# Linear attention into an expert layer on one core: q transposed for two chunks at once, kv in both partition halves, a new order by unit, and two weight semaphores

## The chip, the cores and the metric

The kernel runs on one core of a Trainium2 chip. Times are device microseconds (us) of that core. A program is run several times; runs of one kernel mostly agree within a per cent. A run is called slow when it lies more than 1.5% above the fastest run of the same kernel, and comparisons use fast runs. A single run has no known state, and is used here only for differences well above that. Engines are named as the profile names them: PE is the tensor engine, PEld its weight loads, DVE the vector engine, ACT the scalar engine, POOL the GpSimd engine, SP the engine that issues most loads. In the views, `qo` is a q product, `qtp` the transposes of q and `qT` their copy, `kvp` a k product, `kvc` the evicted kv and `kvtp` its transpose, `kt` and `vtl` the tails of k and v, `wt` the buffer that holds most other tiles, `hp` and `yps` the first and the second layer of an expert tile.

## The reference

```python
# attention: 8 batches, 8 heads, 576 positions, 64 wide, float32
r = relu(x);  phi(x) = concat(r * cos(theta_pos), r * sin(theta_pos))
kv  = einsum('bhsf,bhsd->bhfd', phi(k), v);   z = sum over s of phi(k)
x   = phi(q) @ kv / (phi(q) . z + 1e-6)        # rows: 4608 of 512
# experts: 8, hidden 1024; every row goes to one expert
logits = x @ w_gate;  e = argmax(logits);  gate = softmax(logits)[e]
out[row] = gate * sigmoid(x @ w_output_gate)[e] * (relu(x @ w1[e]) @ w2[e])
```

## The kernel before

The attention part runs over 36 units: a batch has four chunks of 128 positions, and each pair of batches shares a ninth unit for the tails. A group is one such pair, nine units. While the q products of a batch run, k and v of the next one are worked into `kv`. Rows are scattered to their expert's region in memory as the groups end. After that 43 expert tiles of 128 rows follow, each with two layers; the expert of a tile is read from a table into a register.

```python
def load_w(r):                      # weights of the expert ranked r, issued by POOL
    er = GP.value_load(ordi[0:1, r:r + 1], min_val=0, max_val=E - 1)
    if r > 0:
        GP.wait_ge(wsem, 32 * r)    # until all earlier ones have landed
    for d in (GP.dma_start(w1v[:, r], ...), GP.dma_start(w2v[:, r], ...)):
        d.then_inc(wsem, 16)

def k_prep(b, c):                   # k and v step c of batch b
    DVE.tensor_copy(vc[:, :, 0:D], vbuf[b % 2][:, :, c, :])
    ACT.activation(kc[:, 0], src, AF.Relu, scale=cosc[:, c:c + 1])
    DVE.tensor_scalar(kc[:, 1], src, sinc[:, c:c + 1], 0.0, ALU.mult, ALU.max)

def q_prep(b, c):                   # relu of q, heads rearranged
    ACT.activation(qr..., src..., AF.Relu)

def q_tr(b, c):                     # four transposes, one PSUM copy
    ...
    ACT.copy(qT, tp[:])

def layer1(j):                      # expert tile j
    ev = PE.value_load(tcol(0, j), min_val=0, max_val=7)
    wv = PE.value_load(tcol(1, j), min_val=32, max_val=256)
    PE.wait_ge(wsem, wv)
    ...                             # 8 matmuls of 512 columns
    ACT.activation(hs[:], hp, AF.Relu)

for i, (b, c) in enumerate(units):
    q_mm(b, c, ...)
    q_tr(next unit)
    ...                             # k_prep and k_mm of batch b + 1
    if c == len(plan) - 1:          # eviction and transpose at once
        gst["kvc"] = g_evac(b + 1)
        gst["kvT"] = g_tr(b + 1, gst["kvc"])
    elif c == len(plan):
        g_mm(b + 1, gst["kvT"])
        k_prep(b + 2, 0)
    ...
    if c == 2:                      # loads on SP's queue
        load_q(b + 2); load_k(b + 3); load_v(b + 3)
        # even b: also load_tails(g + 1)
```

Of the kernel before, what the change touches and what calls it, by code (L numbers as in the profile page):

```python
# [21 lines left out]
def kernel(  # L22
# [12 lines left out]
    PE = nc.tensor  # L35
# [79 lines left out]
    for qd in range(4):  # L115
        hA = 4 * (qd // 2) + qd % 2
        for ab in range(2):
            h = hA + 2 * ab
            DVE.tensor_copy(wpr[0:64, qd, 32 * ab:32 * ab + 16], wg0[0:64, h, :])
            DVE.tensor_copy(wpr[64:128, qd, 32 * ab + 16:32 * ab + 32],  # L120
                            wg0[64:128, h, :])
# [49 lines left out]
    wsem = tc.alloc_semaphore("wsem")  # L171
    ordi = constp.tile([P, E], I32, name="ordi")

    def load_w(r):
        er = GP.value_load(ordi[0:1, r:r + 1], min_val=0, max_val=E - 1)
        if r > 0:

            GP.wait_ge(wsem, 32 * r)
        for d in (GP.dma_start(w1v[:, r], moe_w1[bass.ds(er, 1)].rearrange(
                      "o (c p) f -> p (o c) f", p=128)),  # L180
                  GP.dma_start(w2v[:, r], moe_w2[bass.ds(er, 1)].rearrange(
                      "o (c p) d2 -> p (o c) d2", p=128))):
            d.then_inc(wsem, 16)
            tc.declare_no_dep(d.ins, group="mm", reason="ranks loaded before")
            tc.add_to_no_dep_group("w", d.ins)
# [16 lines left out]
    r_kvm = Rot(5, 0, 3, 648)  # L202
    r_kc = Rot(5, 2 * 3 * 648, 2, 1024)
    r_u = Rot(6, 0, 2, 1296)
    r_qr = Rot(6, 2 * 2 * 1296, 2, 512)
    r_t = Rot(7, 0, 2, 324)
    r_qT = Rot(7, 2 * 2 * 324, 2, 512)
    r_kvT = Rot(7, 2 * (2 * 324 + 2 * 512), 1, 512)
    r_v = Rot(7, 2 * (2 * 324 + 3 * 512), 3, 520)
# [6 lines left out]
    tabs = [[constp.tile([P, n], I32, name=f"tab{i}_{m}") for m in range(3)]  # L216
# [13 lines left out]
    if True:  # L230
# [6 lines left out]
        tails, kvps, kvms, kcs, qrs, qTs, us, vcs = {}, {}, {}, {}, {}, {}, {}, {}  # L237
# [35 lines left out]
        def k_prep(b, c):  # L273
# [3 lines left out]
            if c < 4:  # L277
                kc = r_kc().rearrange("p (s h d) -> p s h d", s=2, h=H)
                vc = r_v().rearrange("p (h d) -> p h d", d=65)
                DVE.tensor_copy(vc[:, :, 0:D], vbuf[b % 2][:, :, c, :])  # L280
# [10 lines left out]
        def k_mm(b, c):  # L291
# [7 lines left out]
            for hf in range(2):  # L299
                for pr in range(2):  # L300
                    for cs in range(2):
                        for ab in range(2):
                            h = 4 * hf + pr + 2 * ab
                            o = 130 * pr + 65 * cs
                            PE.matmul(kvp[64 * ab:64 * ab + 64, hf, o:o + 65],  # L305
                                      kc[p0:p1, cs, h, :], vc[p0:p1, h, :],
                                      start=(c == 0 and pr == 0 and cs == 0),
                                      stop=(c == 4), skip_group_check=True)


        def g_evac(b):
            kvp = kvps[b]
            kvm = r_kvm().rearrange("p (a w) -> p a w", w=81)
            kvms[b] = kvm
            DVE.tensor_copy(kvm[:, 0:4, 0:65],
                            kvp[:, 0, 0:260].rearrange("p (a w) -> p a w", w=65))
            ACT.copy(kvm[:, 4:8, 0:65],
                     kvp[:, 1, 0:260].rearrange("p (a w) -> p a w", w=65))
            kvc = wk.tile([P, 8, 64], F32, name=f"kvc{b}", tag="kvc", bufs=1)
            DVE.tensor_copy(kvc[:], kvm[:, :, 0:64])  # L320
            return kvc

        def g_tr(b, kvc):
# [5 lines left out]
            kvT = r_kvT()  # L329
            ACT.copy(kvT, tp[:])  # L330
            return kvT.rearrange("p (q w) -> p q w", q=4)

        def g_mm(b, kvT):
            gp = ptr.tile([P, 512], F32, name=f"kvgp{b}", tag="tr")
            for qd in range(4):
                for ab in range(2):
# [4 lines left out]
            DVE.tensor_copy(kvms[b][:, :, 65:81],  # L341
                            gp[:, 0:128].rearrange("p (q w) -> p q w", w=16))


        def q_prep(b, c):
            src = qbuf[b % 2][:, :, c, :] if c < 4 else tails[b // 2, "q"][:]

            qr = r_qr()
            ACT.activation(qr.rearrange("p (r a d) -> p r a d", r=2, a=4),
                           src.rearrange("p (a r) d -> p r a d", r=2), AF.Relu)  # L350
            qrs[b, c] = qr

        def q_tr(b, c):
            qrf = qrs.pop((b, c))
            tp = ptr.tile([P, 512], F32, name=f"qtp{b}_{c}", tag="tr")
            for i in range(4):
                PE.transpose(tp[:, 128 * i:128 * i + 128],  # L357
                             qrf[:, 128 * i:128 * i + 128], ident[:])
            qT = r_qT()
            ACT.copy(qT, tp[:])  # L360
            qTs[b, c] = qT.rearrange("p (q w) -> p q w", q=4)

        def q_mm(b, c, u):
            g = b // 2
            qT = qTs.pop((b, c))
            for hf in range(2):
                qo = pqo.tile([P, 4, 256], F32, name=f"qo{b}_{c}_{hf}", tag="qo")
                for pr in range(2):
                    qd = 2 * hf + pr
                    for ab in range(2):  # L370
                        r0 = 64 * ab
                        lhs = qT[r0:r0 + 64, 2 * pr + hf, :]
                        if c < 4:
                            PE.matmul(qo[:, 2 * ab + pr, 0:162], lhs,  # L374
                                      kvms[b][r0:r0 + 64, 2 * qd:2 * qd + 2, :],
                                      start=True, stop=True)
                        else:
                            for i in range(2):
                                PE.matmul(qo[64 * i:64 * i + 64, 2 * ab + pr, 0:162],
                                          lhs[:, 64 * i:64 * i + 64],  # L380
                                          kvms[2 * g + i][r0:r0 + 64,
# [445 lines left out]
```

## Time and profile before

| | before |
|---|---|
| time, median of 2 runs | 433.11 us (431.85 to 434.36) |
| span of the profiled run (a third run, of 437.43 us), mean granted clock | 435.8 us, 0.913 |
| last q product starts | 195.37 us |
| first expert product starts | 210.73 us |
| last first-layer product starts | 421.97 us |
| median distance of two expert tiles | 4.58 us |

The page of the profile cuts the span into 40 slices, here of 10.9 us. A digit is the busy share of a slice in tenths; the row PEclk is the granted clock of the tensor engine in tenths; the last row is what the DMA engines moved.

```profile
PE   0478988795867799570656989899887999999992
PEclk9999989895998859966596999999999999999997
GB/s 178 298 321 246 245 278 53 318 75 335 39 205 158 159 151 117 184 142 162 121 48 108 129 201 188 191 236 152 185 197 217 74 97 83 53 96 36 50 11 0
```

The reader is to see two regimes. Up to slice 18 is attention with full-clock and cold slices mixed; from slice 23 to slice 39 PE is busy 7 to 9 tenths of the time, mostly 8 or 9, with the granted clock at 9 tenths or more.

### The profile page before, as it was taken

Reading aid. Unit: us, or ns where it says so; the run is one execution under the profiler, and the core shown is the slowest. Engines: PE = TensorE matmul, PEld = TensorE weight load, DVE = VectorE, ACT = ScalarE, POOL = GpSimd, SP = SyncE. Lnnn points to the kernel's source line nnn. Section 1 sums busy time; section 2 is a strip of 40 time slices with the busy share of each in tenths; the row PEclk is TensorE's granted clock in tenths of the full one; section 3 lists DMA queues with packets and bytes.
Section 4 is the critical chain, followed back from the end, with each engine's and each line's share of the span. In section 5 each row is a group of like instructions: output and inputs, shape, how many; then the busy total and the mean of one; then the engine's idle time right before and its main releaser. Section 6 shows DMA issues by size and latency. Waiting matters only on the chain.

```text
span 435.8 us, 9962 instructions
## 1 busy us (share of the span) xinstructions
PE 335.8 (77%) x3468; PEld 222.3 (51%) x3468; DVE 215.3 (49%) x619; ACT 154.5 (35%) x248; POOL 140.8 (32%) x177
## 2 busy tenths in 40 slices
PE   0478988795867799570656989899887999999992
PEld 0467766674756677450323544444444544545441
DVE  4444848574877557773354343343333433433421
ACT  1355767473746467551110212112211112122120
POOL 2001213176314853475343323304241121221211
PEclk9999989895998859966596999999999999999997
DMA  6997892939166587977413699897996232120100
GB/s 178 298 321 246 245 278 53 318 75 335 39 205 158 159 151 117 184 142 162 121 48 108 129 201 188 191 236 152 185 197 217 74 97 83 53 96 36 50 11 0
DMA packets 65374, 66.86 MB, mean 153 GB/s; under 512 B 18350, under 2 KB 57774, under 8 KB 65328
## 3 DMA queue, kind: packets, MB, share of 16 engines
q0 software_dynamic: 17712, 30.98, 32.5%
q1 hardware_dynamic: 47616, 35.25, 29.2%
q8 instruction: 31, 0.51, 0.5%
q14 instruction: 15, 0.12, 0.1%
HBM read 67.61 MB, written 17.22 MB: 195 GB/s over the span
## 4 chain that ended last, share of the span: by engine, by line
DMA 36%; issue 25%; PE 15%; POOL 9%; DVE 7%; SPq 3%; ACT 2%; POOLq 1%; another core or an unknown queue 0%; DVEq 0%; ACTq 0%
DMA xs<-xr,di@1_1635 11%; DMA out_dram<-ysb,sidx 7%; POOL out_dram L666 6%; DMA out_dram<-ysb,xg 6%; PE kvp L305 5%; PE qo L374 4%; DMA xs<-xr,di@3_2587 4%; DMA wt<-in_v_dram 4%; PE qtp L357 2%; POOL xs L467 2%; PE hp L640 2%; DVE wt L386 1%; DMA xs<-xr,di@2_2206 1%; SPq L759 1%; PE kvtp L327 1%
## 5 line engine op out<-in xcount | busy, mean ns | idle before, releaser
L646 ACT ACTIVATE hs<-hp 128x1024 f16<-128x1024 f32 x43 | 44.0, 1023 | 171.4 <-PE hp L640 171.4
L640 PE MATMUL hp<-wt,xts 128*128 x344 | 84.3, 388 | 15.4 <-issue 11.3
L662 DVE TENSOR_SCALAR ysb<-yps,xg 128x512 f32<-128x512 f32 x43 | 32.3, 751 | 128.3 <-PE yps L655 116.7
L655 PE MATMUL yps<-wt,hts 128*128 x344 | 83.0, 385 | 12.4 <-DVE xts L610 8.3
L395 POOL TENSOR_TENSOR xr<-wt,rc 128x1024 f16<-128x1024 f32 (+1 forms) x20 | 37.8, 1890 | 110.2 <-DVE rc L394 105.8
L666 POOL DMA_INDIRECT out_dram<-ysb,sidx x35 | 34.7, 993 | 94.8 <-DVE ysb L662 92.4
L655 PEld LDWEIGHTS <-hts 128*128 128x128 f16 x344 | 33.9, 99 | 54.4 <-DVE xts L610 8.7
L374 PE MATMUL qo<-wt 64*128 64x162 f32 x512 | 51.3, 346 | 12.1 <-DVE wt L386 8.4
L640 PEld LDWEIGHTS <-xts 128*128 128x128 f16 x344 | 33.9, 99 | 51.7 <-issue 18.5
L386 DVE SCALAR_TENSOR_TENSOR wt<-qo,sinc,wt 128x324 f32<-128x324 f32 x72 | 38.4, 553 | 38.0 <-ACT wt L385 36.1
L305 PE MATMUL kvp<-wt 128*64 128x65 f32 x1024 | 40.3, 237 | 20.3 <-ACT wt L288 18.1
L374 PEld LDWEIGHTS qo<-wt 64*128 64x128 f32 x512 | 42.6, 213 | 16.9 <-issue 7.9
L305 PEld LDWEIGHTS kvp<-wt 128*64 128x64 f32 x1024 | 35.9, 149 | 24.6 <-issue 20.8
L385 ACT ACTIVATE wt<-qo,cosc 128x324 f32<-128x324 f32 x72 | 37.7, 530 | 29.9 <-PE qo L374 19.4
L625 DVE COPY hts<-htsp 128x1024 f16<-128x1024 f16 x43 | 29.3, 683 | 1.5 <-issue 1.5
L622 PE MATMUL htsp<-ident,hs 128*128 128x128 f16 x344 | 26.7, 221 | 1.3 <-issue 0.7
L357 PE MATMUL qtp<-ident,wt 128*128 128x128 f32 x144 | 27.5, 321 | 0.0
L288 ACT ACTIVATE wt<-wt,cosc 128x512 f32<-128x512 f32 x32 | 22.5, 722 | 9.2 <-DVE cosc L100 5.1
L607 PE MATMUL xtsp<-ident,xg 128*128 128x128 f16 x172 | 17.5, 227 | 10.7 <-DMA xg<-xs 10.7
L607 PEld LDWEIGHTS <-xg 128*128 128x128 f16 x172 | 13.7, 102 | 21.3 <-DMA xg<-xs 11.0
L610 DVE COPY xts<-xtsp 128x512 f16<-128x512 f16 x43 | 17.9, 416 | 10.9 <-PE xtsp L607 7.5
L360 ACT COPY wt<-qtp 128x512 f32<-128x512 f32 x36 | 21.1, 585 | 5.1 <-PE qtp L357 4.1
(239 smaller groups left out, 327.5 us busy)
## 6 DMA issues: line engine op xcount, KB each, us to landing
wt<-in_moe_w_dram POOLq DMA_DIRECT2D x16, 1024.0 KB
wt<-in_k_dram SPq DMA_DIRECT2D x16, 512.0 KB, 7.1
wt<-in_v_dram SPq DMA_DIRECT2D x16, 512.0 KB, 7.0
wt<-in_q_dram SPq DMA_DIRECT2D x16, 512.0 KB, 6.0
xg<-xs SPq DMA_DIRECT2D x43, 129.0 KB, 2.1
xs<-zt SPq DMA_DIRECT2D x9, 129.0 KB, 3.6
kt<-in_k_dram SPq DMA_DIRECT2D x8, 128.0 KB, 10.1
vtl<-in_v_dram SPq DMA_DIRECT2D x8, 128.0 KB, 6.3
```

The lines of the kernel that those rows point to most:

```text
L305: PE.matmul(kvp[64 * ab:64 * ab + 64, hf, o:o + 65], kc[p0:p1, cs, h, :], vc[p0:p1, h, :], start=(c == 0 and pr == 0 and cs == 0), stop=(c ...
L357: PE.transpose(tp[:, 128 * i:128 * i + 128], qrf[:, 128 * i:128 * i + 128], ident[:])
L374: PE.matmul(qo[:, 2 * ab + pr, 0:162], lhs, kvms[b][r0:r0 + 64, 2 * qd:2 * qd + 2, :], start=True, stop=True)
L385: ACT.activation(t, qo[:, :, 0:81], AF.Copy, scale=cosc[:, c:c + 1])
L386: DVE.scalar_tensor_tensor(u[:, 4 * hf:4 * hf + 4, :], qo[:, :, 81:162], sinc[:, c:c + 1], t, ALU.mult, ALU.add)
L395: GP.tensor_tensor(xr[:, 0:n, 0:DM].bitcast(F16).rearrange("p n (h d) -> p n h d", d=D), u[:, 0:m, 0:64].rearrange("p (n h) d -> p n h d", ...
L607: PE.transpose(xp16[:, kc * 128:(kc + 1) * 128], xg[:, kc * 128:(kc + 1) * 128].bitcast(F16), ident16[:, :])
L640: mm = PE.matmul(hp[:, fh * 512:fh * 512 + 512], xts[:, kc, :], wt[:, bass.ds(ev, 1), kc * F + fh * 512:kc * F + fh * 512 + 512], start=(k ...
L646: ACT.activation(hs[:], hp, AF.Relu)
L655: mm = PE.matmul(yp, hts[:, fc, :], wt[:, bass.ds(ev, 1), 4 * F + fc * DM:4 * F + fc * DM + DM], start=(fc == 0), stop=(fc == 7))
L662: DVE.tensor_scalar(ysb[:], yp, xg[:, DM + 2:DM + 4].bitcast(F32), None, ALU.mult)
L666: d = GP.indirect_dma_start(out=out[:, :], out_offset=bass.IndirectOffsetOnAxis(ap=idx, axis=0), in_=ysb[:], in_offset=None, bounds_check= ...
```

## The change

It has six intents. Relu of q moves into the PSUM copy behind the transposes, which now take two chunks from q's own layout, so one of two ACT passes goes. For that, `kv` must lie in both halves of the partitions, and two DMA copies per batch put it there. The copy of v moves from DVE to ACT. The order by unit changes, so that the eviction of kv ends a unit before its transpose. The late table of the experts is cut into parts. And weights count on two semaphores, so that POOL waits for the last load but one. Smaller edits, such as the places where weights are loaded, are in the kernel but not in these cuts.

```diff
-            GP.wait_ge(wsem, 32 * r)
+            GP.wait_ge(wsem[r % 2], 16 + 32 * ((r - 1) // 2))
...
-                DVE.tensor_copy(vc[:, :, 0:D], vbuf[b % 2][:, :, c, :])
+                ACT.copy(vc[:, :, 0:D], vbuf[b % 2][:, :, c, :])
...
+            SP.dma_start(kvd[0:64, 8:16, :], kvd[64:128, 0:8, :])
+            SP.dma_start(kvd[64:128, 8:16, :], kvd[0:64, 0:8, :])
...
-        def q_prep(b, c):
...
-            ACT.copy(qT, tp[:])
+            ACT.activation(qT[:].rearrange("p q w -> p (q w)"), tp[:], AF.Relu)
...
             ev = PE.value_load(tcol(0, j), min_val=0, max_val=7)
-            wv = PE.value_load(tcol(1, j), min_val=32, max_val=256)
-            PE.wait_ge(wsem, wv)
+            wv = PE.value_load(tcol(1, j), min_val=16, max_val=112)
+            PE.wait_ge(wsem[0], wv)
+            wv = PE.value_load(tcol(3, j), min_val=16, max_val=144)
+            PE.wait_ge(wsem[1], wv)
...
+        kplan = {0: [(1, 1), (1, 2)], 1: [(1, 3), (1, 4), (1, "evac")],
+                 2: [(1, "tr"), (1, "mm")], 3: [(2, 0)], 4: [(2, 1)],
+                 5: [(2, 2), (2, 3)], 6: [(2, 4), (2, "evac")],
+                 7: [(2, "tr"), (2, "mm")], 8: [(3, 0)]}
...
+        def prep_next():            # prepares the step after the one in hand
+            if flat:
+                k_prep(*flat.pop(0))
...
+        k_prep(1, 0)
+        k_do(0, "evac")
+        k_do(0, "tr")
+        q_tr(0)
+        k_do(0, "mm")               # ends with the two copies
+        k_mm(1, 0)
+        prep_next()
...
+            ks = [w for _, w in steps[i] if isinstance(w, int)]
+            if ks:
+                prep_next()
...
+            q_mm(i, u)
+            if i + 1 < NU:
+                q_tr(i + 1)
+            for m, (kb, w) in enumerate(steps[i]):
+                if isinstance(w, int) and w != ks[0]:
+                    prep_next()
+                k_do(kb, w)
...
+            if n in (2, 6):         # n is the unit in its group
+                load_q(bb + 2); load_k(bb + 3); load_v(bb + 3)
+                if n == 2: load_tails(g + 1)
```

## The prediction

> **What bounds the kernel now.** I first cut the span into stretches with the view of windows: the four head-and-batch groups of the attention part (nine chunks each, two batches per group), the hand-over to the experts, and two halves of the expert part.
>
> ```profile
> core 0: us, PE busy (x) PEld busy (x) DVE busy (x) ACT busy (x) POOL busy (x), PEclk, DMA share, GB/s
> 27.90:67.20 39.30, 33.73 (x556) 28.50 (x557) 23.94 (x59) 27.18 (x50) 8.06 (x4) 0.91 0.93 268
> 67.20:114.40 47.20, 36.71 (x566) 30.36 (x566) 31.04 (x82) 27.33 (x52) 20.85 (x24) 0.86 0.61 179
> 114.40:162.00 47.60, 38.12 (x566) 31.86 (x566) 32.43 (x95) 26.81 (x52) 22.89 (x27) 0.82 0.56 149
> 162.00:197.00 35.00, 26.38 (x382) 21.57 (x382) 26.27 (x88) 20.84 (x40) 18.83 (x22) 0.90 0.88 151
> 197.00:237.00 40.00, 18.21 (x92) 8.88 (x93) 17.85 (x67) 4.07 (x6) 16.95 (x26) 0.66 0.40 106
> ```
>
> PE is the busiest engine of every attention group, but the same work (556 to 566 matmul records) costs 39.3 us in one group and 47 in the next two, and the granted clock falls with it. The hand-over at 197 to 237 holds only 18 us of PE work. So PE order bounds the kernel, through its gaps and the slow clock after them. The timeline of PE shows one such gap in the first group:
>
> ```profile
> 38.51 1.15 PE L305 MATMUL kvp<-vtl,ktc 64*64 64x65 f32 x32
> 41.16 0.63 PE L327 MATMUL kvtp<-ident,kvc 128*128 128x128 f32 x4 [1.49 <-DVE kvc L320]
> 41.71 2.17 PE L374 MATMUL qo<-wt 64*128 64x162 f32 x16
> 43.81 1.11 PE L357 MATMUL qtp<-ident,wt 128*128 128x128 f32 x4
> 44.86 0.95 PE L337 MATMUL kvgp<-wpr,wt 128*64 128x32 f32 x16
> 46.30 1.37 PE L374 MATMUL qo<-wt 64*128 64x162 f32 x16 [0.49 <-DVE wt L341]
> ```
>
> PE waits 1.49 us for the eviction of kv, then the next q product takes 2.17 us against 1.37, and its two followers 1.11 and 0.95 against 0.66. That happens once per batch. The hand-over, from the same view (start, duration, engine, line, operation, tiles, count, and in brackets the wait before it):
>
> ```profile
> 195.37 1.34 PE L379 MATMUL qo<-wt 64*64 64x162 f32 x32 [0.67 <-ACT wt L360]
> 207.41 0.61 PE L607 MATMUL xtsp<-ident,xg 128*128 128x128 f16 x4 [10.70 <-DMA xg<-xs]
> ...
> 210.73 3.57 PE L640 MATMUL hp<-wt,xts 128*128 x8 [1.04 <-DVE den@3_2565 L453]
> ...
> 222.74 1.89 PE L640 MATMUL hp<-wt,xts 128*128 x8 [0.22 <-issue]
> ...
> 232.93 3.57 PE L655 MATMUL yps<-wt,hts 128*128 x8 [8.30 <-DVE xts L610]
> ...
> 237.16 1.89 PE L640 MATMUL hp<-wt,xts 128*128 x8
> ...
> 241.73 1.89 PE L640 MATMUL hp<-wt,xts 128*128 x8 [0.29 <-issue]
> ```
>
> PE stands 10.7 us for the first gathered rows (their scatter sits behind an expert's weights), then 8.3 us behind the late table on DVE. In steady state a slot of 128 rows takes 241.73 - 237.16 = 4.57 us. Between the products at 237.16 and 421.97 lie 39 slots, 184.8 us, 4.74 each: 6.6 us of losses. The waits of POOL say where from:
>
> ```profile
> POOL wt L179 <- DMA out_dram<-ysb,sidx: 10.6, 1, 10.6
> POOL wt L179 <- DMA xs<-xr,di@1_1635: 7.6, 1, 7.6
> POOL wt L179 <- DMA out_dram<-ysb,xg: 7.2, 1, 7.2
> ```
>
> POOL blocks before an expert load until the previous one has landed, and scatters and outputs queue up behind it.
>
> **What the Trainium skill says.** "TensorE: Matmul & The Clock Gate", Part 1, says the array runs at half rate after an idle window of about 3.4 us and at full rate again after one busy window. The trace agrees in size (2.17 against 1.37 us, about 3.5 us long), but gaps of only 1.4 to 1.5 us already precede it here. "DMA: Bandwidth & Descriptors", Queues, rings and completion order, says an issuing engine has one ring per DMA engine, consumed in order. The trace agrees: a gather on an empty queue lands in 2.1 us, a v load behind q and k takes a median of 7.0. The first page's specification table calls the ACT, DVE and POOL queues strict FIFO, so program order decides there.
>
> **The change part by part.**
>
> 1. Relu of q moves into the PSUM copy: 32 x 623 ns + 4 x 632 ns = 22.5 us of ACT go. The v copy moves to ACT, 32 instructions; I take the removed 623 ns for the same shape, so 19.9 us come back. DVE loses 32 x 430 ns = 13.8 us. ACT is level: about 28 us per group, against PE's pure work. That work I get from the windows: a mean clock of 0.91 means 18% of the time at half rate, so 39.3 x 0.09 = 3.5 us of the busy 33.7 is slowness, 30.2 remain; likewise 36.7 - 6.6 = 30.1 and 38.1 - 8.6 = 29.5. So 30 us per group. Matmul and transpose counts do not change.
>
> 2. Order. Eviction of kv now stands at the end of a unit, its transpose after the next unit's q product and q transposes (1.31 + 0.59 = 1.9 us of PE work, against the chain of 1.45). So eight gaps of about 1.45 us, 11.6 us, go, and most of the cold stretch after each (0.8 + 0.5 + 0.3 = 1.6 us in the one above). Within the unit of kv transpose and gate product a wait of about 1 us stays, since ACT must do two evictions and the relu first. With about 3 us of small waits, I put a group at 35 to 36 us, the last (one batch of k fewer) at 32.
>
> 3. Two SP copies of kv per batch are new, and q products of odd heads wait for both. On an empty queue: issue 0.5 each plus 2.1 landing plus semaphores, about 3.5 us. They have one unit (3.0 to 3.2 us) to hide in, so 0.5 us per batch is exposed. But they share SP's queue with the loads. At the start, from the timeline of SP:
>
> ```profile
> 21.20 3.10 SPq L242 DMA_DIRECT2D wt<-in_q_dram  x2
> 24.43 2.30 SPq L242 DMA_DIRECT2D wt<-in_k_dram  x2
> 26.78 2.20 SPq L242 DMA_DIRECT2D wt<-in_v_dram  x2
> ```
>
> The first copies come after these, at about 29.3 us, and behind v's bytes (issue plus about 7), so they land near 35.5. First q product: 27.9 before, about 35.6 after; one k product is done meanwhile, so 6.5 us are lost, and a cold restart of 1.5. At later group boundaries the copies stand behind q, k and v of later batches. From the second such burst before (issued from 75.3, drained about 88) I expect landing 12 us after the burst begins, while its unit and the two units after it give about 7.5: 4.5 to 5 us lost at the second boundary, 8 at the first, where nine zero fills (7 us of SP) also stand ahead. At the third only q is left to load; I put 0.5.
>
> 4. Hand-over. Scatters of group 2 now end around unit 33, and the third expert load stands after them, so the first gather can be issued before attention ends. After the last q product I count evictions 1.7, small divisions 1.0, first row copy 0.5, routing to the one-hot 1.8, ranks 0.5: 5.5 us until the first expert product instead of 210.7 - 196.7 = 14.0. Gain 8.5.
>
> 5. The late table is cut over three slots. Per slot PE gives DVE 2.8 us between two second-layer products, of which 2.05 are its own work (0.42 + 0.68 + 0.75 for the two row copies and the output scaling, 0.2 for semaphores), so parts of 3.1, 2.3 and 4.9 us (sums of the row durations) stall PE by 2.3, 1.5 and 4.1: 8 us. Before, 237.16 - 222.74 = 14.4 for one slot, nearly 10 over the pace. Gain near 2 to 3, with the cold stretch.
>
> 6. Weight semaphores: a load waits for the last but one. POOL stops blocking; of 6.6 us lost I give back 5. The third load is also later, still far ahead of its first slot.
>
> Sum, as a time line: first q product 35.6, groups begin near 77, 118 and 154, last q product ends near 186.5 (196.7 before). From there to the end 239 us before; minus 8.5, 2.5 and 5, and about 2 for startup copies I do not see in detail, 221. That gives 407.5 in the profile against 435.8. The median of the timed runs is 433.1 for that profile, 2.7 less, so about 405.
>
> **The rivals.** First, the copies behind loads become the new bound: speaking for it, DMA share 0.93 in group one and the full queue at 21 to 34 us; against it, later groups have share 0.6. If stalls were twice mine, attention would gain nothing and the time would be 420. Second, the reverse: copies slip through and the loads are idle anyway. Then attention ends near 172 and the time is 392. Third, ACT takes PE's place: 28 of 30 us per group, and both halves of a q product now finish together, so evictions begin late. If each of 36 units loses 0.5 us more, that is 18 us: 423. Against it, ACT rows issued back to back start 0.48 to 0.55 us apart, less than their durations. Fourth, the earlier expert start runs into weights not landed: each takes about 16 us (two loads released 16.4 us apart), and loads are now spaced 3 to 4 slots, 14 to 18 us, so outputs queue behind them; five output buffers give 23 us. I allow 3 us.
>
> **Range and chances.** The gain in the hand-over and weights (16 to 18 us, 4%) needs little from attention; attention is 10 us of gain with an error of 12 either way. So 405, 8 in 10 between 391 and 419. Faster by over 2% (below 424.4) 0.92, within 2% 0.07, slower 0.01.
>
> **What would show it.** The kv transpose no longer waits for the eviction; clock per group above 0.93; q products wait for a DMA of kv at the start for about 7 us and at two boundaries for 4 to 8; first expert product 5 to 7 us after the last q product; no POOL wait before weight loads; PE waiting for DVE three times in slots 1 to 4. Wrong would be: q products waiting on ACT or DVE in most units, no wait on the copies, or expert products waiting for weights.

## More of the kernel before

The view of one tile's instructions shows who reads the tables of the experts (count, duration in ns as minimum, median, maximum, and the first and last start in us), here in a window of two expert tiles.

```profile
L629 PEldq TENSOR_LOAD <-tab x2: 300/304/308, 342.3 to 346.9; - x2
L630 PEldq TENSOR_LOAD <-tab x2: 301/304/307, 343.0 to 347.6; - x2
```

PE's own sequencer loads two registers per tile. Each is recorded as 0.30 us, but the second starts 0.70 us after the first.

## The result, and the profile after

The changed kernel takes 488.87 us (488.23 and 489.5), the kernel before 433.11 us: it is slower by 13%. The ratio is 1.1287, with a 95% interval of 1.1133 to 1.1442. Ratios here are the mean time of one kernel's fast runs over the mean of the other's of the same rounds, so not quite the ratio of the medians. The profiled span went from 435.8 to 486.6 us, the granted clock from 0.913 to 0.878.

| stretch of the profiled run | before | after | difference |
|---|---|---|---|
| start to the start of the last q product | 195.37 | 228.09 | +32.7 |
| from there to the first expert product | 15.4 | 11.4 | -4.0 |
| from there to the last first-layer product | 211.2 | 233.1 | +21.9 |
| from there to the end | 13.8 | 14.0 | +0.2 |

So two stretches lost time, one of them the expert part, for which the prediction had only gains. The page after:

```profile
PE   0547857689597677877486777887887788788783
PEclk9977997588799958855568899999999999999999
GB/s 190 297 295 9 141 262 280 58 43 319 316 65 88 337 182 133 9 178 114 109 167 126 76 149 179 177 209 164 185 156 198 111 83 66 55 91 44 43 10 0
```

The expert part stands at 7 and 8 tenths where it was at 8 and 9, at full clock. In attention the DMA row now swings between 9 and 337 GB/s: the loads come in bursts with silence between them. Before, slice 4 of 40 moved 246 GB/s, now 9.

The waits of PE, in all, number of times and longest, from the view of waits:

```profile
PE hp L654 <- issue: 30.2, 30, 1.2
PE kvp L303 <- ACT wt L288: 16.0, 1, 16.0
PE qo L375 <- DMA wt<-wt: 15.0, 3, 6.1
PE kvp L303 <- DMA vtl<-in_v_dram: 11.5, 2, 5.8
...
PE kvtp L326 <- DVE kvc L319: 6.0, 1, 6.0
```

The top line is the expert part: 30 first-layer products were not held by any engine or transfer that the profile shows ("issue"), for a microsecond each. The single 16 us is the start of the program, and is there before the change too. The third, fourth and last are attention: q products that wait for the new copies (`wt<-wt`), k products that wait for the tails of v, and the first kv transpose.

The tables, in a window of two expert tiles, answer the top line:

```profile
L641 PEldq TENSOR_LOAD <-tab x2: 297/300/303, 380.7 to 386.1; - x2
L642 PEldq TENSOR_LOAD <-tab x2: 299/300/302, 381.4 to 386.8; - x2
L644 PEldq TENSOR_LOAD <-tab x2: 295/295/295, 382.1 to 387.5; - x2
```

Each tile now loads three registers, 0.70 us apart, and the products stand behind the last one. From the timeline of PE in the same window (the figure in brackets is the idle time before the first product):

```profile
383.04 1.89 PE L654 MATMUL hp<-wt,xts 128*128 x8 [1.11 <-issue]
...
388.26 1.89 PE L654 MATMUL hp<-wt,xts 128*128 x8 [0.94 <-issue]
```

Before, the same idle time was 0.28 us:

```profile
343.84 1.89 PE L640 MATMUL hp<-wt,xts 128*128 x8 [0.29 <-issue]
...
348.40 1.89 PE L640 MATMUL hp<-wt,xts 128*128 x8 [0.28 <-issue]
```

The Trainium skill, "DMA: Bandwidth & Descriptors", Latency and other measured facts, gives a floor of some 600 ns for a `tensor_load`; 0.70 us from start to start on PE agrees in size; the record of 0.30 us alone does not.

Now SP, in the first group of attention:

```profile
32.20 0.54 SPq L343 DMA_DIRECT2D wt<-wt  x1
...
53.90 0.46 SPq L343 DMA_DIRECT2D wt<-wt  x1
54.40 0.60 SPq L344 DMA_DIRECT2D wt<-wt  x1
55.10 1.14 SPq L242 DMA_DIRECT2D wt<-in_q_dram  x2
56.29 3.15 SPq L242 DMA_DIRECT2D wt<-in_k_dram  x2
59.48 2.15 SPq L242 DMA_DIRECT2D wt<-in_v_dram  x2
61.67 2.80 SPq L258 DMA_DIRECT2D kt<-in_k_dram  x2
64.52 3.40 SPq L261 DMA_DIRECT2D vtl<-in_v_dram  x2
```

From 33.4 to 53.9 us SP issues nothing, because the next instruction in its queue is a copy whose source is not ready. The loads behind it leave at 55.1, where the corresponding ones left from 36.02 us on before the change (not all of that is the copy's doing: see "Copies issued by ACT"); the tails, the last of them, leave at 61.7 to 67.9 and are wanted at 65.9. PE then waits 5.63 us for them, and its first product after that takes 2.00 us, where the same 32 took 1.15. This happens in three groups:

```profile
71.61 2.00 PE L303 MATMUL kvp<-vtl,ktc 64*64 64x65 f32 x32 [5.63 <-DMA vtl<-in_v_dram]
...
89.17 2.49 PE L375 MATMUL qo<-wt,qT 64*128 64x162 f32 x14 [6.07 <-DMA wt<-wt]
...
126.48 2.00 PE L303 MATMUL kvp<-vtl,ktc 64*64 64x65 f32 x32 [5.82 <-DMA vtl<-in_v_dram]
...
172.30 2.00 PE L303 MATMUL kvp<-vtl,ktc 64*64 64x65 f32 x32 [5.80 <-ACT ktc L288]
```

The last of these names ACT, which itself waited for the tail of k.

At the start, ACT stood 5.82 us, until 26.81, for v of batch 1. The eviction of kv of batch 0 was queued behind that, and so were the kv transpose and the first copies.

### The profile page after: what moved, and what is told of

The parts are those of the page before. It is cut to its first block, busy times and chain, and to the rows that moved or that the text cites. A ratio compares the mean times of both kernels' runs of the same rounds, so it can differ in the third digit from the quotient of the medians.

```text
span 486.6 us, 10013 instructions
## 1 busy us (share of the span) xinstructions
PE 353.6 (73%) x3468; PEld 238.5 (49%) x3468; DVE 203.5 (42%) x589; ACT 147.5 (30%) x244; POOL 134.6 (28%) x145
## 4 chain that ended last, share of the span: by engine, by line
issue 29%; DMA 24%; PE 16%; SPq 10%; POOL 8%; DVE 7%; ACT 3%; POOLq 1%; ACTq 0%; DVEq 0%
PE qo L375 8%; POOL out_dram L680 6%; DMA out_dram<-ysb,xg 5%; SPq L242 5%; DMA out_dram<-ysb,sidx 5%; DMA wt<-wt 4%; PE kvp L303 4%; DMA wt<-in_moe_w_dram 3%; PE qtp L358 2%; DMA wt<-in_v_dram 2%; DMA kt<-in_k_dram 2%; SPq L258 2%; DMA vtl<-in_v_dram 2%; DVE wt L390 2%; SPq L261 1%
## 5 line engine op out<-in xcount | busy, mean ns | idle before, releaser
L375 PE MATMUL qo<-wt,qT 64*128 64x162 f32 x512 | 62.8, 375 | 22.2 <-DMA wt<-wt 15.0
L375 PEld LDWEIGHTS qo<-wt,qT 64*128 64x128 f32 x512 | 51.7, 235 | 27.7 <-issue 12.4
L390 DVE SCALAR_TENSOR_TENSOR wt<-qo,sinc,wt 128x324 f32<-128x324 f32 x72 | 36.6, 549 | 49.1 <-ACT wt L387 49.0
L387 ACT ACTIVATE wt<-qo,cosc 128x324 f32<-128x324 f32 x72 | 34.3, 526 | 61.3 <-PE qo L375 54.5
L303 PEld LDWEIGHTS kvp<-wt 128*64 128x64 f32 x1024 | 37.7, 159 | 20.0 <-issue 20.0
L358 PE MATMUL qtp<-ident,wt 128*128 128x128 f32 x128 | 25.2, 329 | 0.0
L303 PE MATMUL kvp<-vtl,ktc 64*64 64x65 f32 x256 | 11.7, 256 | 17.3 <-DMA vtl<-in_v_dram 11.5
L289 DVE TENSOR_SCALAR wt<-wt,sinc 128x512 f32<-128x512 f32 x32 | 15.8, 493 | 18.9 <-PE kvp L303 18.7
L360 ACT ACTIVATE qT<-qtp 128x512 f32<-128x512 f32 x36 | 21.5, 596 | 3.9 <-PE qtp L358 3.7
L634 PEld LDWEIGHTS <-hs 128*128 128x128 f16 x344 | 21.8, 100 | 1.4 <-ACT hs L660 1.0
```

The source lines that it names most:

```text
L303: PE.matmul(kvp[64 * ab:64 * ab + 64, s_ // 2, o:o + 65], kc[p0:p1, cs, 2 * s_ + ab, :], vc[p0:p1, 2 * s_ + ab, :], start=(c == 0 and s_ % ...
L358: PE.transpose(tp[:, 128 * m:128 * m + 128], src, ident[:])
L375: PE.matmul(qos[a][:, m, 0:162], qT[r0:r0 + 64, m, :], kvds[b][r0:r0 + 64, 2 * sl:2 * sl + 2, :], start=True, stop=True)
L387: ACT.activation(t, qos[a][:, :, 0:81], AF.Copy, scale=cosc[:, c:c + 1])
L390: DVE.scalar_tensor_tensor(dst, qos[a][:, :, 81:162], sinc[:, c:c + 1], t, ALU.mult, ALU.add)
L634: PE.transpose(hp16[:, fc * 128:(fc + 1) * 128], hs[:, fc * 128:(fc + 1) * 128], ident16[:, :])
```

## The experiments

Seventeen runs were made. The first four are on the expert part, the last two on both parts, the rest on attention. "Last q" is the start of the last q product in the profiled run (228.09 after the change, 195.37 before), "tile" is the median distance between two expert tiles (5.28 and 4.58). The kernel before ran beside every kernel on the same chip, with medians of 429.5 to 436.3 us.

### One semaphore again

```diff
-            GP.wait_ge(wsem[r % 2], 16 + 32 * ((r - 1) // 2))
+            GP.wait_ge(wsem, 32 * r)
...
-            wv = PE.value_load(tcol(3, j), min_val=16, max_val=144)
-            PE.wait_ge(wsem[1], wv)
```

> The changed kernel with the single weight semaphore of before (one table, one register load and one wait fewer per slot), all else as changed. Theory A: the pace of the expert slots went from 4.57 to 5.28 us because a third register load per slot stands in PE's instruction stream ahead of the first product (about 0.70 us each, 43 slots, 30 us). Then the pace returns to 4.6 and the time falls from 489 to about 460 (up to 465 if the blocking of POOL before weight loads comes back). Rival B: the pace is slow because weights or outputs are late on the DMA queues. Then the pace stays near 5.2 and the time near 489.

Measured: 462.58 us, tile 4.57, last q 231.49. The expert stretch fell from 233.1 to 204.7 us. That is 6.5 us less than before the change, so the rest of the change does gain in that part, as the prediction had it. What the second semaphore puts into PE's stream costs the 28.4 us between.

### The kernel before with one more register load

```diff
             wv = PE.value_load(tcol(1, j), min_val=32, max_val=256)
             PE.wait_ge(wsem, wv)
+            wv2 = PE.value_load(tcol(1, j), min_val=32, max_val=256)
+            PE.wait_ge(wsem, wv2)
```

> The kernel before with nothing changed but a second register load of the same table value and a second wait on the same semaphore in each slot. Theory A: pace 4.57 to 5.27 us, time 433 to about 463. Rival B, or a rival that only a wait on another semaphore costs: pace stays 4.57, time 433.

Measured: 458.24 us against 435.29 for the kernel before on this chip, tile 5.28. The semaphore is the old one and is never short, so it is the load itself. In two tiles:

```profile
L629 PEldq TENSOR_LOAD <-tab x2: 299/303/307, 340.3 to 345.6; - x2
L630 PEldq TENSOR_LOAD <-tab x2: 297/302/307, 341.0 to 346.3; - x2
L632 PEldq TENSOR_LOAD <-tab x2: 294/297/300, 341.7 to 347.0; - x2
```

The spacing of 0.7 us is the same, and the tile grew by 0.70 us.

### Register loads one tile ahead, in the changed kernel

```diff
-            ev = PE.value_load(tcol(0, j), ...)     # and the two others, in layer1(j)
+            ev, wv, wv3 = regs.pop(j)
...
                 layer1(j)
+            if 0 <= j < NSLOT - 1 and j + 1 != EARLY:
+                pre(j + 1)                          # the three loads of the next tile
             if j >= 1:
                 layer2(j - 1, hts)
```

> The changed kernel with the three register loads of the next slot placed between the first and the second layer of the current one; both waits stay where they were. Theory A, if the loads can hide under queued products: the pace falls to 4.6 us or below (the gap before the first product, 0.97, goes to 0 to 0.3), time 449 to 460. Rival: register loads hold PE wherever they stand, pace stays 5.28, time 489.

Measured: 461.27 us, tile 4.55, expert stretch 205.3 us. The loads now run on the sequencer while the eight products of layer 1 are still under way, and most of their time is hidden. It is as good as taking one load away, but no better: three loads are 2.1 us, and the products behind which they hide are 1.9.

### Register loads one tile ahead, in the kernel before

The same edit with two loads, on the kernel before the change.

> The kernel before with its two register loads per slot moved one slot ahead, between the two layers. If the 0.28 us gap ahead of each first product is the tail of those loads, the pace goes from 4.57 to 4.29 and the time from 433 to about 421. If not, 433.

Measured over three rounds: 425.76 us (422.73 to 430.52, the last of them a slow run) against 435.29, ratio of the fast runs 0.9728 with an interval of 0.963 to 0.9827: faster, though not clearly by 2%. The tile is 4.12 us, better than expected. Two loads are 1.4 us and hide behind 1.9. The pace is then PE's own work. So even the two loads that were always there cost 0.46 us a tile. The stops of POOL at the weight loads stay in this version (10.6, 9.4 and 8.0 us among them).

### The start: eviction ahead of the first k and v step

```diff
-        k_prep(1, 0)
         k_do(0, "evac")
+        k_prep(1, 0)
```

> The changed kernel with the first batch's kv eviction placed before the first k and v preparation of batch 1. Theory C: ACT in program order stood 5.8 us on the v load of batch 1 (the v copy is on ACT now) while the kv eviction stood behind it, so PE waited 6.0 us. Then that wait goes to about 1.4, the first copies of kv are issued about 4 us earlier but stand behind the same loads, so the first q product with both halves gains only 0 to 3 us and the time 0 to 4 us. If ACT's order were the whole of the start, 5 to 6 us.

Measured: 487.58 us, last q 231.62. The wait of the first kv transpose went from 6.0 to 1.4 us, but the first complete q product came at 38.71 instead of 39.42: it waited 6.45 us for the copies, not 5.32. The copies stand behind the loads of q, k and v, so an earlier issue only meant a longer wait. The total is within the noise of single runs.

### Tails ahead of the copies

```diff
+            if n == 2 and g + 1 < NG:
+                load_tails(g + 1)
             for m, (kb, w) in enumerate(steps[i]):   # the copies are issued in here
...
-                if n == 2 and g + 1 < NG:
-                    load_tails(g + 1)
```

> The changed kernel with the loads of the k and v tails put ahead of the kv copies and of the q, k, v loads on SP's queue (a batch pair earlier in SP's order by eight DMAs). Theory D: at three boundaries PE waited 5.6 to 5.8 us, plus a cold stretch of 2 to 3, because the tails were issued 12 us too late behind copies that hold SP. Then these three waits go, and the time falls by 15 to 24 us; if the time moves on to the wait for the kv copies, by less than 10.

Measured: 491.58 us, last q 232.13: the main expectation missed. All three waits for tails were gone, so they did come from the place of the tails in the queue, and the waits for copies had taken their place:

```profile
PE qo L375 <- DMA wt<-wt: 23.8, 6, 6.7
```

### Copies issued by ACT

```diff
-            SP.dma_start(kvd[0:64, 8:16, :], kvd[64:128, 0:8, :])
-            SP.dma_start(kvd[64:128, 8:16, :], kvd[0:64, 0:8, :])
+            ACT.dma_start(kvd[0:64, 8:16, :], kvd[64:128, 0:8, :])
+            ACT.dma_start(kvd[64:128, 8:16, :], kvd[0:64, 0:8, :])
```

> The changed kernel with the two kv copies per batch issued from ACT instead of SP. Theory E: the copies cost twice on SP: they hold the loads behind them (100 us of SP's waiting) and stand behind the bytes of earlier loads. From ACT's own queue the waits of q products on the copies (5.3, 6.1, 3.6 us, each with a cold stretch) go to under 1.5 and the loads start earlier: minus 12 to 25 us. Rival: ACT, which is nearly as loaded as PE, now stands waiting for the source of the copy, and loses 1 us or more in each of 8 batches: gain under 8.

Measured: 487.34 us, last q 226.95. The gain is as small as the rival said, and ACT did lose 2.0 to 2.5 us at each of the first four pairs of copies, their issue included. But PE's waits name another reason. The copies met the loads in flight, in eight places:

```profile
PE qo L375 <- DMA wt<-wt: 28.7, 8, 5.0
```

Nor was SP free to issue loads much earlier. The view of SP's own waits, the changed kernel first and this one second:

```profile
SPq L343 <- DVE wt L341: 100.2, 8, 22.8
```

```profile
SPq L242 <- PE qtp L358: 78.1, 11, 16.8
```

With the copies gone from its queue, SP stands at the loads of q instead (L242). The transposes now read q's own load buffer, and the next q can't be loaded over it before the last of them has run; before the change ACT's relu had copied q out earlier. (SP then waited 31.2 us for that relu, in four places.) In the first group the first q load left at 46.36 us here, the first of the tails at 53.20, against 55.10 and 61.67 in the changed kernel and 36.02 and 40.93 in the kernel before. So the copy at the head of the queue accounts for about 9 at most of the 20 us by which these loads are later. Most of the rest is the later start (the first complete q product at 38.41 here, 27.94 before the change); what q's buffer adds no run shows.

The Trainium skill, "DMA: Bandwidth & Descriptors", Issuing engines are not separate DMA queues, says that transfers started by different engines run on the same 16 DMA engines and interleave. The run agrees: another issuing engine did not put the copies in front.

### All three together

> The three together: eviction before preparation at the start, tails first, copies from ACT. If the attention part's loss (32.7 us until the last q product) comes from the order of SP and ACT queues, the last q product starts near 195 to 203 instead of 228, and the time falls to 456 to 464. If it comes from the products themselves (both halves finishing together, evictions late), the last q product stays beyond 212.

Measured: 486.45 us, last q 226.27. The repair that seemed worth 25 to 33 us was worth 2, which is within the noise. From the list of DMA issues (size in KB, median us from issue to landing), the changed kernel and this one:

```profile
wt<-wt SPq DMA_DIRECT2D x16, 162.0 KB, 3.0
```

```profile
wt<-wt ACTq DMA_DIRECT2D x16, 162.0 KB, 7.3
```

The same 162 KB took a median of 3.0 us where the queue in front of most of them had run dry, and 7.3 us in the middle of the loads. Up to here the theory had been that a wait at one place is one loss. The runs say that waits for copies, tails and loads trade places.

### Bursts behind the copies

The next idea was to leave the copies on SP, but let each burst of loads start right after a pair of copies, when the DMA engines are empty: at the start, and in the middle of the group, where the burst moves from unit 6 to unit 7 (after the copies of that unit). The tails lead the burst, the zero fills move from unit 5 to unit 7, and the fix of the start is kept. Parts of it were run alone.

```diff
-        load_q(1); load_k(2); load_v(2)      # ahead of the first copies
...
         k_do(0, "mm")                        # the first copies
+        load_q(1); load_k(2); load_v(2)
...
+            if n == 2 and g + 1 < NG:
+                load_tails(g + 1)
-            if n in (2, 6):
+            if n in (2, 7):
```

> The changed kernel with the bursts of q, k and v loads moved to just after the two copies of kv instead of just before them (start of attention, the burst of every second batch), the tails of the next group loaded first in the burst, the zero fills two units later, and the first k and v work behind the kv eviction. Theory F (a copy issued behind a burst waits for it, whichever queue it is on, and costs about 3 us on idle DMA engines; every such wait also turns the tensor clock down for the following units): the copy waits fall to about 3 us each, the waits for the tails vanish, the last q product starts at 185 to 205 us instead of 228.1, and the time is 445 to 468 us. Rival (the attention part is bound by something else, the ACT and DVE order or the low clock itself, and the waits only take each other's place as in the earlier runs): last q product beyond 215, time 478 or more.

> Only the start is changed: kv eviction ahead of the first k and v work, and the loads of q(1), k(2) and v(2) issued after the copies of the first batch. Theory F: the first complete q product starts at 33 to 36 us instead of 39.4 and the first copy wait is about 3 us; whether the later waits stay (copies of the next batches, three tails waits) this run can say: if they stay as they are, 481 to 486 us in all; if all slide earlier together, the gain is 4 to 7 us. Rival: the loads now come late, the next batch waits for k and v instead, and nothing is gained (487 to 492).

> Only the bursts in the middle are moved behind the copies (and tails first, zero fills later); the start stays as in the changed kernel. Theory F: the first wait stays (first complete q product at about 39 us), the waits for tails at 71, 126 and 172 us vanish, later copy waits are 3 us or less; last q product at 195 to 212 instead of 228.1, time 455 to 475. Rival: the waits move to other loads (q of the next batch, k), time 482 or more.

Measured: 482.69 us for all of it (last q 223.55), 484.47 for the start alone (224.06), 490.8 for the middle alone (230.6). The start did what it should: the first complete q product came at 34.39 us, after a wait for copies of 2.48, and the total is 4.4 us lower, which is no more than chips differ by. The full version and the middle alone ended where their rivals had said. In the full version the waits for copies fell to 3.6 us in all, and still nothing was won. What had come up in their place is to be seen in the timeline of ACT:

```profile
57.15 0.60 ACT L360 ACTIVATE qT<-qtp 128x512 f32<-128x512 f32 x1
57.62 0.73 ACT L288 ACTIVATE ktc<-kt,cosc 128x512 f32<-128x512 f32 x1
66.13 0.62 ACT L280 COPY wt<-wt 128x512 f32<-128x512 f32 x1 [7.78 <-DMA wt<-in_v_dram]
66.65 0.72 ACT L288 ACTIVATE wt<-wt,cosc 128x512 f32<-128x512 f32 x1
67.28 0.93 ACT L387 ACTIVATE wt<-qo,cosc 128x324 f32<-128x324 f32 x2
68.10 0.59 ACT L360 ACTIVATE qT<-qtp 128x512 f32<-128x512 f32 x1
```

and in that of PE:

```profile
68.75 2.74 PE L375 MATMUL qo<-wt,qT 64*128 64x162 f32 x16 [6.91 <-ACT qT L360]
```

At 58 us ACT has come to the copy of v of batch 3. Its product is in unit 8, but the change prepares every step one ahead, in unit 6, and across the border of two batches that means a v whose load was issued only at 55.55. ACT stands for 7.78 us, and the evictions of q and the relu of the next q, which need nothing of v, stand behind it. After the first load ACT waited for v 36.1 us in seven places, and PE for ACT's `qT` 22.6 us in five.

### Every k and v step prepared in its own unit

One call less, on top of the version above: the step in hand is prepared at the start of its own unit.

```diff
         k_mm(1, 0)
-        prep_next()
```

> The previous version with the bursts behind the copies, and in it each k and v step is prepared on ACT and DVE at the start of its own unit, not one step ahead. Theory G: the tensor engine is late because ACT and DVE, which work in order, stand at the first k and v step of a batch whose load was issued only 4 to 6 units before (7.8 us for v of batch 3, with the relu of the next q transposes queued behind it), and the lead of the step ahead buys nothing. Then the ACT waits for the v load (36.1 us, 7 times) fall to under 15 us, the waits of the tensor engine for qT (22.6 us, 5 times) to under 8 us, last q product at 200 to 212 us instead of 226, time 458 to 470. Rival: the load itself lands too late for the tensor engine, whichever engine stands for it, so the same time is then lost at the k and v products: last q product beyond 218, time 474 or more.

Measured: 457.24 us, last q 197.13. That is better than the range expected, and 25.5 us less than with the step ahead. The waits of ACT for v in this version, over the whole run (the first is at the start of the program, as before):

```profile
ACT L280 <- DMA wt<-in_v_dram: 14.1, 1, 14.1
...
ACT wt L280 <- DMA wt<-in_v_dram: 4.9, 3, 2.8
```

PE's wait for `qT` is down to 0.9 us, and the granted clock is 0.911, about that of the profiled run of the kernel before.

### k and v of a burst ahead of q

```diff
                 if bb + 3 < B:
                     load_k(bb + 3)
                     load_v(bb + 3)
+                if bb + 2 < B:
+                    load_q(bb + 2)
```

> The version before with k and v of batch b+3 loaded ahead of q of batch b+2 in each burst. Theory G with late loads: k and v are wanted 4 to 6 units after the burst, q only 6; each burst of 3.1 MB takes some 10 us, so v lands about 3.5 us earlier: 3 bursts on the path, 5 to 12 us less than the version before. Rival: q is then the late one, and the gain is under 3 us.

Measured: 457.95 us, last q 198.01. Nothing was gained, as the rival said. After the start (one wait of 3.6 us, until 27.74) ACT no longer waited for v; that q was the late one instead, as the rival had it, no wait shows.

### The step ahead alone, and v on DVE alone

The first takes the one call out of the changed kernel and leaves everything else as it is; the second puts the copy of v back on DVE.

> The changed kernel with one line taken out: the k and v steps are prepared in their own unit, not one step ahead; copies, bursts, tails and start stay as the change has them. If the step ahead on the in-order engines is the whole of what was lost in the attention part: last q product at 197 to 206 us instead of 228.1, time 457 to 468. If both parts are needed (the copies at the head of the queue hold the tails back whatever ACT does, as the earlier runs suggest): the three waits for tails stay, last q product at 212 to 226, time 473 to 487.

> The changed kernel with the copy of v back on DVE, as before the change. If it is ACT alone that must not stand at the v load: ACT no longer waits for v at the start (kv transposes wait under 2 us instead of 6.0) and the time falls by 4 to 12 us. If not (tails and copies are what it waits for, and DVE stands at v in its place): 484 to 492 us.

Measured: 491.95 us (last q 234.72) and 490.88 us (230.32). Neither helps alone. With the steps in their own unit two of the three waits for tails vanish, but the copies still stand behind the bursts, 21.2 us in six places. So neither the start and bursts (6 us, at most) nor the step ahead (nothing) is the cause by itself; both together were worth 31.6 us (488.87 to 457.24). These two runs carry a flaw: PE also stopped at k products for 6.6 and 7.2 us with no cause in the profile, of which more below.

### What was learned, put together

The repaired attention, one semaphore, and its two register loads moved a tile ahead.

> The version before with one weight semaphore and the two register loads of an expert tile moved a tile ahead between the layers. From the earlier runs (26.3 us for the one semaphore, 27.6 us for the loads moved ahead, not both in full): 27 to 33 us less than the version before, so 420 to 440 us where theory G holds, against 432 before the change.

Measured over three rounds: 408.39 us (406.99 to 410.63) against 432.84 for the kernel before on the same chip, ratio 0.9416 with an interval of 0.9323 to 0.9509. That beats both kernels and the range expected. That it is within 4 us of what had been predicted for the change is a coincidence: it is another program. Last q is 194.22, the tile 4.12. From the timeline of PE, one tile and the start of the next:

```profile
301.97 1.89 PE L655 MATMUL hp<-wt,xts 128*128 x8
303.70 1.89 PE L670 MATMUL yps<-wt,hts 128*128 x8
305.43 0.39 PE L615 MATMUL xtsp<-ident,xg 128*128 128x128 f16 x4
305.65 0.61 PE L630 MATMUL htsp<-ident,hs 128*128 128x128 f16 x8
306.10 1.89 PE L655 MATMUL hp<-wt,xts 128*128 x8
```

No bracket is left: PE goes from product to product without a pause.

### The same with two semaphores and three loads ahead

> The fastest version so far (408.4 us, ratio 0.942), but with the two weight semaphores of the change and their three register loads moved a tile ahead. If the loads hide fully, the second semaphore brings what the prediction gave it, up to 5 us: 402 to 408. If a third load a tile ahead still costs (the earlier run with three loads ahead stood at a pace of 4.5 to 4.6 us per tile, this version with two at 4.28): 44 tiles by 0.2 to 0.3 us, 416 to 424.

Measured over three rounds: 446.34 us (443.58 to 448.12), ratio 1.0254 (1.0195 to 1.0313): worse than either range. The tile is 4.54, against 4.12 with two loads (not the 4.28 of the expectation). From the view of waits and the timeline:

```profile
PE yps L676 <- issue: 11.6, 32, 1.3
```

```profile
341.56 1.89 PE L661 MATMUL hp<-wt,xts 128*128 x8
343.70 1.89 PE L676 MATMUL yps<-wt,hts 128*128 x8 [0.25 <-issue]
```

Three loads outlast the layer that hides them, and the second layer waits. That is 0.41 us by 43 tiles, 17.6 us, and about the 16.8 by which the expert stretch is longer (205.1 against 188.3). Of these the view shows 11.6 as waits; it leaves out waits under 0.15 us. Another 17.3 us lie ahead of the last q product (211.48 against 194.22), where the two programs are the same; this is not explained. Some of it are stops of PE without a cause in the profile. They come in k products, about 0.7 us apart. The two kernels with the same attention (last q 194.22 and 211.48) ran on two chips: on the first no profiled run has such stops, on the second all three have 5.6 to 7.2 us of them. But the chip alone does not decide: on a third chip two kernels had 5.2 and 6.1 us, two others 1.9.

## Why the prediction was wrong

It said 405 us (391 to 419) and the time is 488.87. In the profile it said 407.5 and the span is 486.6, 79.1 us more. These divide into 44.0 before the end of the last q product (186.5 said, 228.09 + 2.44 = 230.5 measured), 3.4 in the hand-over (5.5 said, 239.45 - 230.53 = 8.9 measured) and 31.7 after it (215.5 said, 486.6 - 239.45 = 247.15 measured).

Step 6 failed in what it left out. "POOL stops blocking" came true: POOL's waits before weight loads are 2.3 us for outputs and 0.9 for scatters, where single ones had been 10.6. But the second semaphore has to be waited for by PE too, with its own table entry and its own register load in every tile. The diff shows those two lines, and no term of the sum had them. Shown by three runs: taking the load out gives 28.4 us back in the expert stretch; putting a load into the kernel before makes its tile 5.28 us; moving the loads a tile ahead gives the time back with both semaphores in place (expert stretch 205.3). This is 28.5 of the 31.7 us (the version with one semaphore takes 218.6 from the first expert product on). The remaining 3.1 are the small terms. The 5 us that step 6 gave to the second semaphore show in no run: with the loads hidden the expert stretch is 205.3, with one semaphore at 204.7.

Step 3 failed in direction, not only in size. It asked how late the loads make the copies. At the start it said 35.6 us for the first q product (39.42 measured), for the waits at the next boundaries 8, 4.5 to 5 and 0.5 (6.07, none and 3.57 measured; at the second PE stood 0.38 us for DVE). So that part was roughly right in sum, not one by one. It never asked how late the copies make the loads. SP's queue is in order, a copy at its head waits for its source, and all loads behind it wait too: SP stood 20 us there in the first group. Three waits for tails of 5.6 to 5.8 us, with the cold stretch after each, come from that (they went with the tails ahead, and with the copies on ACT), and the bursts after each silence then delay the next copies. It also left out that q's load buffer comes free later, so that with the copies out of the way SP stood 78.1 us for the transposes. Both can be read from the changed kernel: from the order of its calls, and from what its transposes read.

Step 1 was right for totals and wrong for order. ACT is level (147.5 us busy, 154.5 before). But it is not indifferent what ACT does when: with v on ACT and prepared one step ahead across batches, ACT can stand at a load with the relu of q behind it. This was masked in the changed kernel (only the 5.8 us at the start show) and appeared as soon as the copies were out of the way. The 25.5 us between two versions that differ in one call show it.

Step 2 was right in its mechanism: kv transposes no longer wait for their eviction except once at the start, where the order was other (10.1 us in seven places before, 6.0 in one after; three new waits, 3.9 us in all, are for DVE's routing). Its lengths were too short. It said 35 to 36 us for a group; in the fastest version, in a stretch with the full clock, the same work takes 40 us:

```profile
110.00:150.00 40.00, 33.12 (x570) 27.79 (x568) 28.45 (x83) 25.00 (x52) 20.52 (x18) 1.00 0.85 241
```

PE is busy 33.1 us there, not the 30 that I had worked out from the mean clock, and the rest is some 7 us of small waits, where 3 were allowed. So the 10 us that attention was to gain were not there: the repaired attention has its last q product at 194 to 198 us (on one chip; at 211.48 on another, not explained), the kernel before at 195.4. Of the 44.0 us before the end of the last q product, 32.1 went when bursts and step ahead were changed (it ends at 198.46 there), which is what steps 3 and 1 had left out; the other 12.0 are about what step 2 took too short.

Step 4 gained 5.1 us of 8.5: the first gather was indeed earlier, but PE still waited 3.79 us for it and 2.00 for the routing. Step 5 was close: it said stalls of 2.3, 1.5 and 4.1 us by the late table, the trace has 2.70, 0.79 and 2.60.

Of the rivals, the first came nearest in mechanism (copies behind loads become the bound, 420 us; the third was nearer in number by luck, 423) and was still 69 us short, as it too had no term for the loads behind the copies or for the registers. The range was too narrow because all of its terms were about the parts that the prediction had thought of.

What stays open: what the later release of q's buffer costs; how much of the 44 us is to be charged to the cold clock and how much to the waits themselves, as no run changed the one without the other; and the stops without a cause.

## What to carry to other kernels

Count every instruction that a change adds to each engine's own stream, register loads and waits included: one of 0.70 us in a loop of 43 cost 28.4 us, and two of them moved behind running matmuls became free. When a pass that copied data out of a load buffer is removed, ask what now holds the buffer, and for how long. When a transfer is put into an in-order queue, ask what stands behind it while it waits for its source, and do not let an in-order engine come to an instruction whose load was issued only just before, if others wait behind it. Where waits trade places from one run to the next, repair all of the loop before judging any part of it.

## What the Trainium skill lacked or had wrong

- "DMA: Bandwidth & Descriptors", Latency and other measured facts, has the floor of a register load, but not whether it is hidden. Here each load holds PE's stream for 0.70 us (record 0.30 us). Two of them hide behind eight products of 1.89 us in all, three don't (tile 4.12 and 4.54 us). In front of the products a third one costs its full 0.70, the first two together 0.46.
- The same page, Issuing engines are not separate DMA queues, is right, but has no size: 162 KB from one half of the partitions to the other land after a median of 3.0 us in the changed kernel, mostly behind an empty queue, and after 7.3 us among loads of 3.1 MB a burst, issued by another engine.
- "TensorE: Matmul & The Clock Gate", Part 1, names an idle window of about 3.4 us, but not how full a window must be for the clock to come back. In the changed kernel the last four full units of attention ran at 2.5 to 2.9 us for 16 products that take 1.37 warm, with idle gaps of only 0.69 us before most of them. From 204.65 to 228.09 us PE was busy 80% of the time and the granted clock stayed at 0.50, while the stretch of the fastest version shown above has 83% at 1.00. So a stream once cold can stay so.
- No page has the stops at k products, about 0.7 us apart, that no engine or transfer in the profile explains: 5.6 to 7.2 us in each of three runs on one chip, none in three on another.
